# A new searched issue order, MLP partial sums split by token group, and dense matmuls in four column tiles, in an attention + token-mixing MLP kernel on one Trainium2 core

## The chip, the cores and the metric

The kernel runs on one core of one Trainium2 chip. The metric is the device time of one execution in microseconds (us). The time before is the median of 3 runs. One further execution was profiled, and its trace is what the numbers below come from.

## The reference, cut to what matters

There are 2048 tokens with 512 channels, in bf16. A vector `c` gives six modulation vectors `sa, ca, ga, sb, cb, gb`. Then:

```python
h = layernorm(x) * (1 + ca) + sa
qkv = h @ wqkv                      # 512 -> 1536; 32 heads of 16
p = softmax(mask(q @ k.T / 4))      # causal, window of 256 tokens
x = x + ga * ((p @ v) @ wo)
h = layernorm(layernorm(x) * (1 + cb) + sb)
u = gelu(h.T @ w1 + b1)             # the MLP mixes tokens: 2048 -> 1792
x = x + gb * (u @ w2 + b2).T        # 1792 -> 2048
```

The MLP contracts over tokens. Its first product needs the rows of all 2048 tokens, but a part of the sum over tokens can be formed as soon as those tokens have left attention.

## The kernel before, in words

**Groups.** Tokens are handled in four groups G of 512 (four tiles of 128). For each group: layer norm, projection to queries, keys and values (`proj0`, `proj`), attention (`attention`), output projection, residual and the two layer norms (`post`), which leave the tiles `hb`, the input of the MLP.

**Attention.** There are 75 chunks (`chunks`). A chunk is one group of score matmuls on TensorE (tiles `pss` and `psb`, in four row tiles of 32), two exponentials on ScalarE (`et<-pss` over 1536 columns and `et<-psb` over 512), and masks on VectorE (`et<-et,maskt`). The tile `pss` has one buffer, so the scores of a chunk wait until the long exponential of the chunk before is done. When all chunks of a unit (8 heads, 256 queries) are there, `sums` issues the value sums and the sums of the weights (`po`, 52 matmuls for most units), each matmul in one of four column tiles of 32 (tile form 128*32). `finish` takes the logarithm and the exponential of the sums (`lz`, ScalarE) and multiplies (`OT`, VectorE).

**Dense matmuls** use the full array (128*128) and 512 columns: projections (`pk`, `pq`, `pv`), output projection (`pa`), first MLP product (`pu`, in the program also `pu2`), second MLP product (`py`). In the planner a change between row tiles, column tiles and the full array costs `SWITCH` = 0.107 us, by the class `cls` of an operation.

**MLP.** `w1` has 14 column blocks `fc` of 128, loaded in pairs. `partials` sums each of the 14 blocks over the token tiles 0 to 7 (eight matmuls into one PSUM tile) once groups 0 and 1 have left `post`, and copies the sum into `part`. `tail` and `mlp1` then add the token tiles 8 to 15 (`pu2`, 8 matmuls for each block, 112 in all). Eight PSUM tiles are open at a time, so blocks 8 to 13 start when earlier ones have been emptied. Then come gelu and the second product: 16 output tiles with 14 matmuls each (`py`). This kernel's first eight token tiles of a pair of blocks are one load of 512 KB (`w1p`), the other eight a second one (`load_w1(pair, 1)`, operation `w1h`) into the same buffer, once the partial sums that read the first are done. The 14 loads of `w2` (`e_w2`, 512 KB each, tiles `w2r`) start when attention's buffers are released.

**Order.** Every operation is an `Op` with an engine, a planned cost and dependencies. `run_schedule` issues all of them in the order of the list `ORDER` (L60), with engines from `CHOSEN` (L114); issue order is the program order of each engine. All loads but three early ones are issued by SyncE (SP). The operation `w2` has a planned cost of 0.0 and issues its 14 loads in a row.

**Opening.** TensorE runs 16 matmuls of zeros (`warm`, written into `pss`) around the modulation matmuls (`ps_fm`) and the transposes of the first two token tiles, before the first key projection.

All operations are recorded through one helper, so the profile gives them line L234, and they are told apart by their tiles.

Of the kernel before, what the change touches and what calls it, by code (L numbers as in the profile page):

```python
# [9 lines left out]
ACT = mybir.ActivationFunctionType  # L10
# [3 lines left out]
P = 128  # L14
# [12 lines left out]
PART_A = 3  # L27
PART_AT = 20.0
# [3 lines left out]
X_READY = [3.0, 3.75, 11.7, 12.0]  # L32
MOD_READY = [4.7, 6.7, 6.9, 7.4]
W_READY = [8.35, 9.25, 9.25, 11.0, 14.0]
# [17 lines left out]
ZSCALE = 2.0 ** -32  # L52

# [59 lines left out]
]  # L113
CHOSEN = {  # L114
    "ACT": [
        48, 50, 72, 74, 95, 1017, 1034, 1039,
    ],
    "DVE": [
# [4 lines left out]
    ],  # L123
    "POOL": [
        712, 714,
    ],
}
BATCH = True
XT_AFTER = -0.7
W1_AFTER = 2.0  # L130
AV_POS = 0.2
LZ_POS = 0.0
# [4 lines left out]
class Op:  # L137
# [5 lines left out]
    def __init__(self, name, eng, cost, emit, deps=(), pos=0.0, cls=None, alloc=None, ready=0.0, extra=0.0, behind=()):  # L143
# [5 lines left out]
        self.done = None  # L149
        Op.count += 1  # L150
        self.n = Op.count

# [1201 lines left out]
```

## Time and profile before

| | us |
|---|---|
| median of 3 runs | 255.73 (255.32 to 256.43) |
| profiled execution, its own time | 258.61 |
| its span, first to last instruction | 256.8 |
| TensorE busy | 241.1 (94% of the span), 3427 matmuls |
| ScalarE busy | 179.9 (70%) |
| VectorE busy | 200.6 (78%) |
| GpSimd busy | 133.0 (52%) |
| mean granted TensorE clock | 0.993 |

The span has an opening up to 12.5 us, attention with ScalarE busy nearly throughout until about 175 us, and a last stage to 256.8 us in which TensorE runs dense matmuls without a break. Matmuls overlap, so their durations (380 ns) are longer than the step from one to the next; steps are read from their starts.

### The profile page before, as it was taken

The numbers are of one execution on the slowest core, as the hardware profiler recorded it, in microseconds if no ns is written. First come the engines' busy times: TensorE is split into PE (matmuls) and PEld (weight loads), VectorE is DVE, ScalarE is ACT, GpSimd is POOL, SyncE is SP. The second block draws the span as 40 slices with busy tenths as digits, with TensorE's granted clock in tenths as the row PEclk, the third lists the DMA queues.
The fourth block names the chain that finished last, engine by engine and source line by source line (L and its number), as shares of the span: only waits on it lengthen the run. The fifth ranks groups of instructions, "written<-read, shape, count | busy, mean of one in ns | idle before, by whom it ended". The sixth has DMA issues, their size and how long they took to land.

```text
span 256.8 us, 8133 instructions
## 1 busy us (share of the span) xinstructions
PE 241.1 (94%) x3427; PEld 122.2 (48%) x3427; DVE 200.6 (78%) x392; ACT 179.9 (70%) x255; POOL 133.0 (52%) x237
## 2 busy tenths in 40 slices
PE   7988989899998999979999999999999999999994
PEld 2665635444443454434545454446444444444443
DVE  4589999998899999998658879799869864444442
ACT  4399999999999999998999999998138510000000
POOL 8288977999999897896914389190000000000000
PEclk9999999999999999989999999999999999999999
DMA  7998360246254400060030003351899601111111
GB/s 222 326 349 252 12 80 3 42 114 159 61 120 60 116 3 3 9 182 0 5 92 14 3 3 84 106 142 37 326 332 387 232 22 41 58 48 41 41 43 41
DMA packets 41341, 27.02 MB, mean 105 GB/s; under 512 B 11992, under 2 KB 37208, under 8 KB 41304
## 3 DMA queue, kind: packets, MB, share of 16 engines
q1 hardware_dynamic: 41008, 25.97, 36.2%
q8 instruction: 27, 0.44, 0.7%
q10 hardware_dynamic: 296, 0.53, 0.6%
q14 instruction: 10, 0.08, 0.1%
HBM read 22.03 MB, written 2.10 MB: 94 GB/s over the span
## 4 chain that ended last, share of the span: by engine, by line
PE 61%; POOL 12%; DVE 10%; ACT 8%; issue 4%; DMA 3%; SPq 0%; DVEq 0%; POOLq 0%
PE pu L234 20%; PE py L234 19%; PE po L234 7%; ACT et L234 6%; PE pss L234 6%; POOL VT L234 4%; PE pa L234 3%; DVE et L234 3%; POOL xn L234 3%; POOL KT L234 2%; PE pk L234 2%; DMA w1p<-in_B_w_dram 2%; PE pv L234 2%; ACT lz L234 1%; DVE vb L234 1%
## 5 line engine op out<-in xcount | busy, mean ns | idle before, releaser
L234 ACT ACTIVATE et<-pss 128x1536 bf16<-128x1536 f32 x75 | 110.8, 1477 | 3.3 <-PE psb L234 1.7
L234 PE MATMUL pu<-hb,w1p 128*128 128x512 bf16 x224 | 52.6, 380 | 0.0
L234 DVE TENSOR_TENSOR et<-et,maskt 128x1024 bf16<-128x1024 bf16 (+2 forms) x79 | 48.5, 628 | 2.7 <-ACT et L234 2.6
L234 PE MATMUL py<-guT,w2r 128*128 128x512 bf16 (+1 forms) x238 | 48.7, 366 | 0.5 <-DVE otile L234 0.5
L234 ACT ACTIVATE et<-psb 128x512 bf16<-128x512 f32 x75 | 46.9, 626 | 0.0
L234 PE MATMUL pss<-QT,KT 32*128 32x64 bf16 (+3 forms) x720 | 30.0, 232 | 6.6 <-ACT et L234 5.0
L234 PEld LDWEIGHTS <-w2r 128*128 128x128 bf16 x238 | 23.3, 98 | 26.0 <-issue 0.7
L234 PE MATMUL po<-et,VT 128*32 128x64 bf16 (+3 forms) x960 | 32.3, 237 | 1.0 <-DVE kb L234 0.6
L234 PEld LDWEIGHTS <-w1p 128*128 128x128 bf16 x224 | 20.4, 98 | 25.0 <-issue 2.5
L234 PE MATMUL po<-et,ones_bd 128*32 128x256 bf16 (+3 forms) x624 | 32.0, 271 | 0.0
L234 POOL TENSOR_SCALAR KT<-kb,mask_par 128x512 bf16<-128x512 bf16 (+1 forms) x38 | 27.4, 732 | 7.2 <-ACT kb L234 5.8
L234 DVE TENSOR_TENSOR otile<-py,xr 128x512 bf16<-128x512 f32 (+1 forms) x17 | 11.2, 660 | 25.3 <-PE py L234 25.2
L234 PEld LDWEIGHTS <-KT 32*128 32x128 bf16 x960 | 15.8, 93 | 31.1 <-issue 28.9
L234 PE MATMUL psb<-QT,KT 32*128 32x64 bf16 (+3 forms) x240 | 29.5, 232 | 0.0
L234 PEld LDWEIGHTS <-VT 128*32 128x32 bf16 x960 | 19.6, 97 | 12.9 <-issue 10.7
L234 POOL TENSOR_SCALAR xn<-x,rs,nm 128x512 bf16<-128x512 bf16 x24 | 22.8, 951 | 1.4 <-DVE h L234 0.5
L234 DVE BATCH_NORM_STATS2 st<-x 128x6 f32<-128x512 bf16 x32 | 21.4, 682 | 2.2 <-DMA x<-in_A_x_dram 2.1
L234 PE MATMUL pk<-h1T,wqkv 128*128 128x256 bf16 (+2 forms) x108 | 21.3, 326 | 0.6 <-DVE vb L234 0.5
L234 PEld LDWEIGHTS <-wqkv 128*128 128x128 bf16 x164 | 13.8, 99 | 13.4 <-issue 6.0
L234 DVE TENSOR_TENSOR OT<-po,lz 128x256 bf16<-128x256 f32 x32 | 13.3, 416 | 8.2 <-ACT lz L234 8.2
L234 PE MATMUL pv<-wqkv,h1T 128*64 128x256 bf16 (+1 forms) x112 | 17.2, 321 | 0.4 <-DVE OT L234 0.4
L234 PE MATMUL pa<-wod,OT 128*128 128x512 bf16 x64 | 17.0, 380 | 0.4 <-DVE kb L234 0.2
(99 smaller groups left out, 324.1 us busy)
## 6 DMA issues: line engine op xcount, KB each, us to landing
w1p<-in_B_w_dram SPq DMA_DIRECT2D x14, 512.0 KB, 5.0
w2r<-in_B_w_dram SPq DMA_DIRECT2D x14, 512.0 KB, 7.8
x<-in_A_x_dram SPq DMA_DIRECT2D x16, 128.0 KB, 5.2
wmod<-in_w_mod_dram SPq DMA_DIRECT2D x4, 512.0 KB, 8.6
out_dram<-otile SPq DMA_DIRECT2D x15, 128.0 KB, 1.7
wqkv<-in_A_wqkv_dram SPq DMA_DIRECT2D x4, 256.0 KB, 4.9
vs<-vb SPq DMA_DIRECT2D x24, 32.0 KB, 3.0
wmod<-in_w_mod_dram ACTq DMA_DIRECT2D x2, 256.0 KB, 3.7
```

Of the source, the lines that this page charges most:

```text
L234: ins = call(*args, **kwargs)
```

## The change

1. **Order.** `ORDER` and `CHOSEN` are new lists. The planned costs of many operations on VectorE and GpSimd are lower (0.77 for 0.88 of a normalization on GpSimd). More operations can go to either engine: `kk`, `vp`, `vo`, `xn`, `n2` and `hb`. In the program this moves 8 normalizations `xn`, 6 `hb`, 8 copies into `VT` and 6 splits into `KT` from GpSimd to VectorE, and 6 scalings of `h1T` and 6 multiply or add steps of `h` the other way.
2. **Partials by token groups.** For the first `EARLY` = 10 blocks `fc`, the token tiles 0 to 3 are summed first and copied into `part` (`pe`); later the tiles 4 to 7 are summed and added (`pd`, VectorE, 10 new additions). Blocks 10 to 13 still sum eight tiles at once. `w1` is loaded in 28 quarters of 256 KB (tiles `w1s`, `w1r`) in place of 14 halves.
3. **Four column tiles.** Dense operations of the stage get the class of the value sums. Those in a run of at most `NEAR_RUN` = 7 operations beside a value sum are issued by `mm` as four matmuls of 32 columns, 163 dense matmuls in all (652 small ones).
4. **Smaller edits.** 12 warming matmuls for 16, ten of them at the very start; the first transposed tiles are both copied by ScalarE; the zeros of `VT[2]` are two SP transfers instead of four GpSimd fills.

The diff, cut to its core (`ORDER` and `CHOSEN` are left out):

```diff
+    runs = []
+    for o in (ops[i] for i in ORDER if "PE" in ops[i].engs):
+        if not runs or runs[-1][0].cls != o.cls:
+            runs.append([])
+        runs[-1].append(o)
+    for run in runs:
+        sums = [n for n, o in enumerate(run) if o.name == "AV"]
+        if run[0].cls == "AV" and sums:
+            for a, b in zip([-1] + sums, sums + [len(run)]):
+                if b - a <= NEAR_RUN:
+                    for o in run[a + 1 : b]:
+                        o.tiled = True
...
+    def mm(dst, lhsT, rhs, start, stop):
+        if not Op.quad:
+            te.matmul(dst, lhsT=lhsT, rhs=rhs, start=start, stop=stop, skip_group_check=True)
+            return
+        for j in range(4):
+            rows = slice(32 * j, 32 * j + 32)
+            te.matmul(
+                dst[rows], lhsT=lhsT[:, rows], rhs=rhs, start=start, stop=stop, tile_position=(0, 32 * j), skip_group_check=True,
+            )
...
-    warms = [op("warm", "PE", 0.86 if i < 4 else 0.43, lambda e, i=i: e_warm(e, 2, i == 0), pos=-7, cls="D", ready=1.4 if i < 4 else 4.8)
-             for i in range(8)]
+    warms = [op("warm", "PE", 0.86, lambda e: e_warm(e, 2), pos=-7, cls="D", ready=1.4) for i in range(6)]
...
+    def load_w1(pair, quarter):
+        first = quarter in (0, 2) or (quarter == 1 and pair < EARLY // 2)
+        name = f"w1{'s' if first else 'r'}{pair}"
+        t = box["w1" if first else "B"].tile([P, 4, 2 * P], BF, name=name, tag=name)
+        dma.dma_start(out=t[:], in_=w1_v[:, 4 * quarter : 4 * quarter + 4, 2 * P * pair : 2 * P * (pair + 1)])
+        w1t[pair, quarter] = t
...
+        for fc in range(EARLY):
+            pos = start_of(2) + EARLY_AT + fc * EARLY_STEP
+            early[fc] = group(fc, 0, [loads[fc // 2, 0], *done[:4]], pos, True)
+            if fc % 2:
+                load(fc // 2, 1, [early[fc - 1], early[fc]], pos + 0.5)
...
+            if fc < EARLY:
+                g = group(fc, 4, [loads[fc // 2, 1], *done[4:]], pos, False)
+            else:
+                g = group(fc, 0, [loads[fc // 2, 0], loads[fc // 2, 1], *done], pos, True)
             part_ops.append(g)
-            if fc % 2 == 1:
-                second[fc // 2] = op("w1h", "SP", 1.35, lambda e, fc=fc: load_w1(fc // 2, 1), deps=[g], pos=pos + 0.5, extra=W1_AFTER)
+            if fc % 2:
+                second[fc // 2] = [
+                    load(fc // 2, 2, part_ops[-2:], pos + 0.5),
+                    load(fc // 2, 3, [released] + (part_ops[-2:] if fc >= EARLY else []), max(pos, start_of(NG) - 10.0) + 0.6),
+                ]
...
-                o = op("u", "PE", 0.431, e_u, deps=done[sc : sc + 2] + prev + guard + [part_ops[PART_A], second[fc // 2]],
-                       pos=pos + (later if sc == NT - 2 else 0.01), cls="D", alloc="od" if kind == "od" and sc == lo else None)
+                o = op("u", "PE", 0.431, e_u, deps=done[sc : sc + 2] + prev + guard + second[fc // 2],
+                       pos=pos + (later if sc == NT - 2 else 0.01), cls="AV", alloc="od" if kind == "od" and sc == lo else None)
```

More of the change, by code (lines that the diff above doesn't have):

```diff
@@ L26 @@
 NPART = 14
-PART_A = 3
-PART_AT = 20.0
+EARLY = 10
+EARLY_AT = 6.0
+EARLY_STEP = 1.4
 KQ_AT = -3.0
@@ L284 @@
     nc.gpsimd.memset(ones_bd[KB:P, DH : 2 * DH], ZSCALE)
+    nothing = const.tile([P, D], BF, name="nothing")
+    nc.vector.memset(nothing[:], 0.0)
     late = ctx.enter_context(tc.tile_pool(name="late", bufs=2))
@@ L310 @@
     modw = tc.alloc_tile_pool(name="modw", bufs=1, side="right")
-    warm = modw.tile([P, D], BF, name="warm")
-    nc.vector.memset(warm[:], 0.0)
+    warm = nothing
     wmod = modw.tile([P, ND, 6 * D], BF, name="wmod")
@@ L439, with e_warm @@
     box = {}
-    def e_warm(e, n, first):
+    def e_warm(e, n):
         if "warm" not in box:
@@ L492, with dense @@
     fms[0].frees = [o_fm]
-    def dense(name, pieces, emit, deps, pos, cls="D", alloc=None, ready=0.0):
+    fms[1].deps += warms
+    def dense(name, pieces, emit, deps, pos, cls="AV", alloc=None, ready=0.0):
         first = None
@@ L523, in e_bce @@
                 ve.tensor_copy(out=dst[:], in_=box["bc", v][:])
[L525 removed]
+        a, z = dense(f"bc{v}", [0.435] * 2, e_bc, [o_rep], 9.0 + n, cls="D", alloc="od", ready=22.0)
         b = op(f"bce{v}", "DVE", 0.6, e_bce, deps=[z], pos=9.0 + n)
@@ L625, in normed @@
                 o.ready = X_READY[i]
-            xn_ops = [op("xn", "DVE", 0.33, lambda e, i=i: e_xn(e, i), deps=[st], pos=base + 0.5) for i in own]
+            xn_ops = [op("xn", "DVE", 0.36, lambda e, i=i: e_xn(e, i), deps=[st], pos=base + 0.5) for i in own]
             def e_tr(n):
@@ L672, in e_hh @@
                         e_h(e, 2 * i + 1)
-                    hs[half].append(op("h1T", {"ACT": 0.94, "DVE": 0.7}, 0.9, e_hh, deps=[z, o_fm], pos=base + 1.5))
+                    hs[half].append(op("h1P", {"ACT": 0.94, "DVE": 0.7}, 0.9, e_hh, deps=[z, o_fm], pos=base + 1.5))
                     a.frees = hs[half][-1:]
@@ L730, in e_mm @@
                     w0 = (1 - n) * D + g8 * P
-                    te.matmul(
-                        box["kq", g8][:, n, :], lhsT=wqkv[:, dc, w0 : w0 + P], rhs=h1T[:, dc, cols],
-                        start=(dc == 0), stop=(dc == ND - 1), skip_group_check=True,
+                    mm(
+                        box["kq", g8][:, n, :], wqkv[:, dc, w0 : w0 + P], h1T[:, dc, cols],
+                        (dc == 0), (dc == ND - 1),
                     )
@@ L810, in proj0 @@
             f(p)
-        zeros[2] = [
-            op("z", "POOL", 0.93, lambda e, n=n: po.memset(VT[2][:, 2 * n : 2 * n + 2, :, :], 0.0), deps=k_done[0, 1][-1:], pos=1.0 + n)
-            for n in range(4)
-        ]
+        zeros[2] = []
+        for n in range(2):
+            zeros[2].append(op("z2", "SP", 2.6, lambda e, n=n: dma.dma_start(
+                out=VT[2][:, 4 * n : 4 * n + 4, :, :].rearrange("p b a d -> p b (a d)"),
+                in_=nothing[:].unsqueeze(1).to_broadcast([P, 4, D]),
+            ), deps=zeros[2] + k_done[0, 1][-1:], pos=14.0 + n, ready=30.0, extra=1.0))
         proj_last[0] = op("fence", "SP", 0.0, lambda e: None, deps=last, pos=13.0, extra=-2.0)
@@ L866, in e_q @@
                 for dc in (2 * n, 2 * n + 1):
-                    te.matmul(
-                        box["q", g8][:], lhsT=wqkv[:, dc, g8 * P : (g8 + 1) * P], rhs=h1T[:, dc, :],
-                        start=(dc == 0), stop=(dc == ND - 1),
+                    mm(
+                        box["q", g8][:], wqkv[:, dc, g8 * P : (g8 + 1) * P], h1T[:, dc, :],
+                        (dc == 0), (dc == ND - 1),
                     )
@@ L886, in e_k @@
                 for dc in (2 * n, 2 * n + 1):
-                    te.matmul(
-                        box["k", g8][:], lhsT=wqkv[:, dc, D + g8 * P : D + (g8 + 1) * P], rhs=h1T[:, dc, :],
-                        start=(dc == 0), stop=(dc == ND - 1),
+                    mm(
+                        box["k", g8][:], wqkv[:, dc, D + g8 * P : D + (g8 + 1) * P], h1T[:, dc, :],
+                        (dc == 0), (dc == ND - 1),
                     )
@@ L924, in e_v @@
                 for dc in (2 * n, 2 * n + 1):
-                    te.matmul(
-                        box["v", tb][:], lhsT=h1T[:, dc, tb * P : (tb + 1) * P], rhs=wqkv[:, dc, 2 * D : 3 * D],
-                        start=(dc == 0), stop=(dc == ND - 1),
+                    mm(
+                        box["v", tb][:], h1T[:, dc, tb * P : (tb + 1) * P], wqkv[:, dc, 2 * D : 3 * D],
+                        (dc == 0), (dc == ND - 1),
                     )
@@ L956, in v @@
             vx = op("vx", "SP", 1.05, e_vx, deps=[ve_op], pos=pos, extra=0.1)
-            own = op("vo", "POOL", 0.97, lambda e: e_vp(e, True), deps=[ve_op] + war + zeros[r3], pos=pos)
-            b = op("vp", "POOL", 0.97, lambda e: e_vp(e, False), deps=[vx, own] + war + zeros[r3], pos=pos)
+            own = op("vo", {"POOL": 0.78, "DVE": 0.45}, 0.78, lambda e: e_vp(e, True), deps=[ve_op] + war + zeros[r3], pos=pos)
+            b = op("vp", {"POOL": 0.78, "DVE": 0.45}, 0.78, lambda e: e_vp(e, False), deps=[vx, own] + war + zeros[r3], pos=pos)
             ring("vb", 2, ve_op, b)
@@ L979, in e_wo @@
                 for g in (2 * n, 2 * n + 1):
-                    te.matmul(
-                        box["wo", tl][:], lhsT=OT[r2][g][:, tl * P : (tl + 1) * P], rhs=wod[:, g, :],
-                        start=(g == 0), stop=(g == ND - 1),
+                    mm(
+                        box["wo", tl][:], OT[r2][g][:, tl * P : (tl + 1) * P], wod[:, g, :],
+                        (g == 0), (g == ND - 1),
                     )
@@ L992, in post @@
             a.frees = [x_ops[tl]]
-        engine, shifted = ({"POOL": 0.88}, True) if G < POOL_POST else ({"DVE": 0.33}, False)
+        engine, shifted = ({"POOL": 0.77, "DVE": 0.35}, True) if G < POOL_POST else ({"DVE": 0.34}, False)
         st = norm_ops("l2", lambda i: xres[4 * G + own[i]], [[x_ops[tl]] for tl in own],
@@ L1024, in e_w1 @@
         box["A"] = ctx.enter_context(tc.tile_pool(name="partA", bufs=1, side="right"))
-    def load_w1(pair, half):
-        own = half == 1 and pair >= NPART // 2
-        name = f"w1p{pair}_{half}" if own else f"w1p{pair}"
-        t = box["B" if own else "w1"].tile([P, 8, 2 * P], BF, name=name, tag=name)
-        dma.dma_start(out=t[:], in_=w1_v[:, 8 * half : 8 * half + 8, 2 * P * pair : 2 * P * (pair + 1)])
-        w1t[pair, half] = t
+    def load_w1(pair, quarter):
[4 more added lines that the diff above has]
+        w1t[pair, quarter] = t
     def w1s(sc, fc):
-        return w1t[fc // 2, sc // 8][:, sc % 8, (fc % 2) * P : (fc % 2 + 1) * P]
+        return w1t[fc // 2, sc // 4][:, sc % 4, (fc % 2) * P : (fc % 2 + 1) * P]
     part_ops = []
@@ L1040, in partials, with load, e_rel @@
         opened = op("w1", "SP", 0.0, e_w1, deps=mod_ops + [o_fm, masks_built], pos=start_of(1) + 2.0, extra=-2.0)
-        loaded = []
+        loads = {}
+        chain = []
+        def load(pair, quarter, deps, pos):
+            name = f"w1{'abcd'[quarter]}"
+            o = loads[pair, quarter] = op(name, "SP", 1.3, lambda e: load_w1(pair, quarter), deps=deps, pos=pos, extra=W1_AFTER)
+            return o
+        def e_rel(e):
+            wpool.release()
+            box["B"] = ctx.enter_context(tc.tile_pool(name="partB", bufs=1, side="right"))
@@ L1042, in partials @@
         for n in range(NF // 2):
-            loaded.append(op("w1l", "SP", 2.6, lambda e, n=n: load_w1(n, 0), deps=loaded[-1:] or [opened],
-                             pos=start_of(1) + 3.0 + 2.0 * n, extra=W1_AFTER))
+            chain.append(load(n, 0, chain[-1:] or [opened], start_of(1) + 3.0 + 2.0 * n))
         done = [hb_ops[G][tl] for G in range(2) for tl in range(4)]
-        for fc in range(NPART):
-            at = start_of(2) + PART_AT
-            pos = at + fc * (start_of(NG) - PART_END - at) / NPART
-            def e_p(n, fc=fc):
+        released = op("rel", "SP", 0.0, e_rel, deps=[proj_last[NG - 1]], pos=start_of(NG) - 12.0, extra=-2.0)
@@ L1051, in e_p, with group @@
+        def group(fc, lo, deps, pos, first):
+            hi = 8 if first and fc >= EARLY or not first else 4
+            def e_p(n):
                 if n == 0:
                     box["p", fc] = bank([P, D], F32, "pu")
-                for sc in (2 * n, 2 * n + 1):
-                    te.matmul(
-                        box["p", fc][:], lhsT=w1s(sc, fc), rhs=hb[sc][:], start=(sc == 0), stop=(sc == 7),
-                    )
-            def e_pe(e, fc=fc):
-                if fc == PART_A:
-                    wpool.release()
-                    box["B"] = ctx.enter_context(tc.tile_pool(name="partB", bufs=1, side="right"))
-                    for pair in range(NPART // 2, NF // 2):
-                        load_w1(pair, 1)
-                part[fc] = box["A" if fc < PART_A else "B"].tile([P, D], F32, name=f"part{fc}")
-                copy(e, part[fc][:], box["p", fc][:])
@@ L1067, in partials @@
-            behind = [proj_last[NG - 1]] if fc >= PART_A else []
-            a, z = dense("p", [0.431] * 4, e_p, [loaded[fc // 2]] + done + behind, pos, alloc="od")
-            g = op("pe", {"ACT": 0.5, "DVE": 0.6}, 0.6, e_pe, deps=[z] + part_ops[-1:], pos=pos)
-            a.frees = [g]
-            part_ops.append(g)
-            if fc % 2 == 1:
-                second[fc // 2] = op("w1h", "SP", 1.35, lambda e, fc=fc: load_w1(fc // 2, 1), deps=[g], pos=pos + 0.5, extra=W1_AFTER)
+                for sc in (lo + 2 * n, lo + 2 * n + 1):
+                    mm(
+                        box["p", fc][:], w1s(sc, fc), hb[sc][:], (sc == lo), (sc == hi - 1),
+                    )
@@ new lines, in e_pe @@
+            def e_pe(e):
+                if first:
+                    part[fc] = box["A" if fc < EARLY else "B"].tile([P, D], F32, name=f"part{fc}")
+                    copy(e, part[fc][:], box["p", fc][:])
+                else:
+                    ve.tensor_tensor(out=part[fc][:], in0=box["p", fc][:], in1=part[fc][:], op=ALU.add)
+            a, z = dense("p", [0.431] * ((hi - lo) // 2), e_p, deps, pos, alloc="od")
+            g = op("pe" if first else "pd", {"ACT": 0.5, "DVE": 0.6} if first else "DVE", 0.68, e_pe,
+                   deps=[z] + ([released] if fc >= EARLY else []) + ([] if first else [early[fc]]), pos=pos)
@@ new lines, in group @@
+            a.frees = [g]
+            return g
+        early = {}
+        for fc in range(EARLY):
[3 more added lines that the diff above has]
+                load(fc // 2, 1, [early[fc - 1], early[fc]], pos + 0.5)
+        for pair in range(EARLY // 2, NF // 2):
+            load(pair, 1, [released], start_of(NG) - 11.0 + pair - EARLY // 2)
+        for fc in range(NF):
+            at = start_of(3)
+            pos = at + fc * (start_of(NG) - PART_END - at) / NF
+            if fc < EARLY:
+                g = group(fc, 4, [loads[fc // 2, 1], *done[4:]], pos, False)
+            else:
+                g = group(fc, 0, [loads[fc // 2, 0], loads[fc // 2, 1], *done], pos, True)
+            part_ops.append(g)
+            if fc % 2:
[3 more added lines that the diff above has]
+                ]
```

44 lines of the change are left out of this document (23 added, 21 removed), and 119 rows, old and new, of tables (CHOSEN, ORDER).

## The prediction

> **What bounds the kernel now.** I read the profile by stage: first the chain of work that ended last, in order of time, for the end.
>
> ```profile
> 181.83 22.88 PE pu L234 x106
> 204.71 46.87 PE py L234 x224
> ```
>
> From the last score matmuls on, TensorE is the bound: 112 `pu2` and 238 `py` matmuls must all run there, in program order, and nothing else is late. So whatever holds one of them up delays the end by as much. Next the busy times by stretches (columns: busy time of PE, weight loads, VectorE, ScalarE, GpSimd; then granted clock, share of the DMA engines, GB/s).
>
> ```profile
> 20.00:113.00 93.00, 84.46 (x1655) 43.54 (x1653) 89.33 (x175) 92.31 (x125) 82.56 (x140) 1.00 0.36 75
> 113.00:116.50 3.50, 3.27 (x56) 1.77 (x55) 3.47 (x7) 2.95 (x5) 2.72 (x5) 0.51 0.56 157
> 116.50:172.00 55.50, 54.99 (x995) 27.48 (x994) 44.09 (x79) 54.09 (x74) 33.07 (x55) 1.00 0.20 52
> 178.00:182.00 4.00, 4.00 (x20) 1.86 (x19) 2.98 (x7) 1.19 (x4) 0.00 (x0) 1.00 0.63 217
> 182.00:186.00 4.00, 4.00 (x21) 1.78 (x19) 3.46 (x10) 1.10 (x3) 0.00 (x0) 1.00 0.91 343
> 186.00:190.00 4.00, 4.00 (x20) 1.84 (x19) 3.19 (x9) 1.33 (x3) 0.00 (x0) 1.00 1.11 319
> 190.00:194.00 4.00, 4.00 (x21) 1.79 (x19) 2.47 (x5) 2.22 (x4) 0.00 (x0) 1.00 1.08 366
> 194.00:202.00 8.00, 8.00 (x39) 3.64 (x38) 6.95 (x15) 5.34 (x8) 0.00 (x0) 1.00 1.05 386
> 202.00:204.00 2.00, 2.00 (x11) 0.93 (x10) 1.44 (x5) 0.98 (x2) 0.00 (x0) 1.00 0.45 169
> ```
>
> Up to 113 us ScalarE is busy 92.31 of 93: attention runs at its pace and cannot run faster. From 178 to 203 us the DMA engines are full: the loads of `w2`. Last, SP's own timeline, where the transfers are issued, and the tile `w1p`:
>
> ```profile
> 177.93 2.90 SPq L234 DMA_DIRECT2D w2r<-in_B_w_dram  x5
> 184.88 0.99 SPq L234 DMA_DIRECT2D w1p<-in_B_w_dram  x2
> 185.92 8.25 SPq L234 DMA_DIRECT2D w2r<-in_B_w_dram  x9
> ...
> DMA to landing us min/median/max: 4.0/5.0/7.9
> ```
>
> The last two pieces of `w1` go between the fifth and the sixth load of `w2`. The later of them holds blocks 10 and 11 and is first used by the 67th of the 112 `pu2`, 46 before their end: 204.71 - 46 x 0.2155 = 194.8 us. Issued by 185.87, and landing at most 7.9 later (193.8), it is in time by about 1 us. (0.2155 is the step of dense matmuls: 22.88 / 106 = 0.216.)
>
> **The change, part by part.** All sums are against the profiled span of 256.8; what they give is added to the median of 255.73.
>
> *Order of the transfers.* In the changed program's instruction order SP's last loads stand so:
>
> ```
> w1r6                x1    (last quarter of pair 6)
> w2r0, w2r1          x14
> w1s6                x1    (third quarter of pair 6)
> w1s4                x1    (third quarter of pair 4: blocks 8 and 9)
> ```
>
> On TensorE the 61st `pu2` (block 8, token tile 8) loads `w1s4`. Call T the end of the value sums, when attention's buffers are released (before: 177.77, `w2` issued at 177.93). When is `w1s4` wanted? After T: 6 `pu2` (1.29) and a class switch, about 0.1 until the last `OT` (1.5 in all; before, `pa` started 1.74 after T), 8 `pa` (1.72), 54 `pu2` (11.64): T + 14.9. When does it land? Before, the rows above add up to 8.4 MB, the 14 loads of `w2` and the two of `w1`, the last bytes at 202 + 0.34 MB / 386 = 202.9, which is T + 25.1. After, two pieces of 0.26 MB take the place of two of 0.52, so 0.52 MB less at 319 GB/s, 1.6 us: T + 23.5, and an estimated 0.5 until the counter arrives: T + 24.0. TensorE stands still for 9.1 us, and 52 `pu2` and all `py` are queued behind it. Lower bound, all 7.86 MB at 386 GB/s with the first bytes at T + 1.6: T + 22.0, 7.1 us. Upper bound: `w1r6`, issued just ahead, takes 0.8 us of the same engines and the counter 1 us: 10.4. I take 9.1, from the same transfers of the same stage. Could it be hidden? No: in this stage TensorE has no other work, and its program order is fixed.
>
> *Clock after the standstill.* The granted clock was 0.51 from 113 to 116.5 us, after TensorE had stood idle for 1.72 us; 3.5 us at 0.51 cost 1.7 us of work. After 9 us of standstill the same should come: +1.7, from +0.5 (if it ends early) to +3.4 (two such stretches, an estimate). The Trainium skill, "TensorE: Matmul & The Clock Gate", Part 1, says that the clock is judged in free-running windows of about 3.4 us and returns only after a busy one, so resumed work pays the rest of one window too. By that the term would be up to 3.4 and the sum 266.1; the one stretch here, 3.4 us long, agrees with the window's length.
>
> *Attention.* Switches between row tiles, column tiles and full array fall from 189 to 157 between the first and the last scores, by counting both orders; at 0.11 us (8 `pu` between score groups took 1.83, and 8 x 0.2155 is 1.72) TensorE saves 3.5 us. But ScalarE paces here: 75 long exponentials issued every 1.34 us when queued, 75 short ones at 0.48, 64 `lz` at 0.26 and 0.31; all that stays. What can be won are ScalarE's gaps, the largest 1.27 us at 113.9 and 117.2, in the stretch of half clock, where TensorE had little to do (two score groups with nothing between). The early sums of 40 dense matmuls land around there, so I take half of it and some: -0.8, between -2.0 (gaps gone; the work between successive scores now averages 2.03 us in the last 24 chunks, 2.13 before, where the exponentials need about 2.07) and +1.5 (one such gap elsewhere, as the chunks 30 and 31 now have only 1.30 us of work each).
>
> *VectorE and GpSimd.* The ten added `pd` cost 0.69 each (as `part<-pu`), 6.9 us, in a stage where VectorE is busy 44.09 of 55.50. Normalizations of 0.95 on GpSimd become 0.41 on VectorE, copies of 0.51 about 0.42 (as the 256-column cast into `kb`). Both stay below ScalarE's pace; their risk is in the +1.5. The two SP transfers of zeros and 14 more `w1` issues of 0.4 to 0.6 us stand ahead of exchanges `vs`, which attention needs only a group later; taken at 0.
>
> *Four column tiles.* 52 value-sum matmuls (13 groups of four, 2560 columns in all per tile) took 1.21 with a switch, so 1.10: the groups run side by side at 1.07 us for 2560 columns. 512 columns in four tiles then cost 0.216, as one dense matmul does: 0.
>
> *Opening.* The first key projection started at 10.49, behind six warming matmuls; its input was there at 9.36 (8.50 + 0.86). Without these, 1.1 us could go, less 0.45 for the second copy behind the first on ScalarE: -0.6, at best -1.2 (one projection fewer before the first scores). But up to 10.07 the warming matmuls stepped at 0.43, half rate; if full rate comes later without them, the 16 matmuls ahead of the first scores cost 1 us more and the next ones too: +1.5.
>
> *After the last scores.* 104 value-sum matmuls are left instead of 156, 13 groups of four less (1.1 us), and 132 dense ones for 130 (+0.4): -0.7, up to 0 if `pa` waits.
>
> Sum: -0.6 - 0.8 - 0.7 + 9.1 + 1.7 = +8.7; 255.73 + 8.7 = **264.4** (the profiled span would be 265.5).
>
> **Rivals.** *The load is in time, faster.* If `w1s4` lands before T + 14.9, only -2.1 is left: 253.6. By the rates above 4.5 MB, under nine loads of `w2`, have moved by then, so it would have to pass at least five. Against it: before, the two `w1` pieces behind five loads of `w2` landed up to 7.9 after their issue, though other pieces needed 4.0, so they queued. For it: no row shows a queue of fourteen.
> *It overtakes in part.* SP paused from 180.83 to 184.88 after five loads, so it lets few be open (in the order each waits for a counter used eight loads before). If `w1s4` is issued when the eighth `w2` load is in (T + 13) and needs the median of 5.0, it lands at T + 18: 3.1 us, and a shorter cold stretch: 255.73 - 2.1 + 3.1 + 0.9 = 257.6. The full DMA engines from 186 to 202 speak against it.
> *Column tiles are dear.* If each of the 163 showed one weight load (0.098 us), 16 us more on TensorE, half of it in chunks where ScalarE waits: 264.4 + 8 = 272. Against it: 960 small loads for `po` with the same mean (97 ns), hidden. The Trainium skill, "TensorEngine Tiling (Array Packing)", Restrictions and Gotchas, says that column tiling excludes the fast weight load, which speaks against this part; by this trace the loads of both forms take the same 97 to 98 ns.
>
> **How the numbers follow.** The forecast has 0.84, the partial overtaking 0.07, the load in time 0.04, dear column tiles 0.05. Combining the terms' bounds as independent gives about -3 and +4 around 264.4: 260.8 to 268.3, which holds nine tenths of the forecast's own cases, near 8 in 10 of all. 0.5% (1.3 us) is about what a measurement of this kernel tells from no change. Faster: the load in time, 0.04. Same: the lower edge of the overtaking, 0.03. Slower: 0.93.
>
> **What would show it.** Right: a standstill of TensorE of 7 to 10 us some 15 us after the last value sums, ended by the landing of `w1s4`, a clock near 0.5 behind it, and `py` starting near 214. Right for the rest: no gap of 1 us in ScalarE between 20 and 170, four column tiles of 512 columns stepping at 0.216. Wrong: TensorE without a gap from the last scores to the end, or `w1s4` landing before its `w2` neighbours.

## The result, and the profile after

The changed kernel takes **268.49 us** (median of 4 runs, 268.02 to 269.78), the kernel before 255.9 (255.32 to 256.43): a ratio of 1.05, 95% interval 1.0455 to 1.0546. It is slower, as forecast; the forecast of 264.4 was 4.1 us short, and its range ended 0.2 us below the result. The profiled execution took 268.85 us, with a span of 267.1 us.

TensorE's timeline behind the last value sums (start, duration, group; in square brackets the idle time ahead of the group and what ended it):

```profile
188.22 4.05 PE L256 MATMUL pu<-hb,w1r 128*128 128x512 bf16 x17
202.10 1.89 PE L256 MATMUL pu<-hb,w1s 128*128 128x512 bf16 x4 [9.84 <-DMA w1s<-in_B_w_dram]
203.78 1.06 PE L256 MATMUL pu<-hb,w1r 128*128 128x512 bf16 x2
...
214.87 10.31 PE L256 MATMUL py<-guT,w2r 128*128 128x512 bf16 x46
```

The value sums end at T = 177.41. The `pu` in need of `w1s4` is the next in order at 192.26, which is T + 14.85; it starts at 202.10, T + 24.7. The two `pu` of 203.78 span 1.06 us where a pair spans 0.59 at full clock. SP's queue shows why it waited:

```profile
175.32 0.37 SPq L256 DMA_DIRECT2D w1r<-in_B_w_dram  x1
177.56 12.39 SPq L256 DMA_DIRECT2D w2r<-in_B_w_dram  x14
190.91 3.45 SPq L256 DMA_DIRECT2D w1s<-in_B_w_dram  x2
```

The two late loads are issued at 190.91 and 192.26, over 13 us behind the first of `w2`: in the trace, eight transfers are open at a time, and each further issue comes when the load eight before it has landed (the issue of 192.26 behind a landing at 192.25). The loads of `w2` land one after the other, 1.36 us apart, and `w1s4` lands at 202.05, 9.8 us after its issue. The same stage by stretches (columns as before: TensorE, weight loads, VectorE, ScalarE, GpSimd, then granted clock, DMA share, GB/s):

```profile
180.00:200.00 20.00, 12.21 (x56) 5.39 (x55) 12.94 (x29) 6.83 (x13) 0.00 (x0) 0.88 1.03 373
200.00:202.00 2.00, 0.00 (x0) 0.00 (x0) 0.00 (x0) 0.00 (x0) 0.00 (x0) 0.50 0.15 37
202.00:205.00 3.00, 2.90 (x7) 1.04 (x8) 0.00 (x0) 0.00 (x0) 0.00 (x0) 0.50 0.00 0
205.00:218.00 13.00, 12.95 (x60) 5.93 (x60) 9.58 (x20) 5.78 (x8) 0.00 (x0) 0.99 0.01 3
```

The DMA engines are full (1.03) until about 200 us; in the last 2 us of the wait only the rest of the two late loads moves (0.15). The clock is half from 195.0 (0.88 over 20 us is about 5 us at half) to 205.2: 10.2 us, the last 3.1 of them with work, which cost 1.6.

Last, the end of attention in both kernels, 21 us up to about 1 us before the last long exponential, before and after:

```profile
151.30:172.30 21.00, 21.00 (x338) 9.96 (x330) 19.01 (x34) 20.67 (x29) 14.26 (x20) 1.00 0.40 101
```

```profile
150.00:171.00 21.00, 18.64 (x450) 10.52 (x450) 20.41 (x36) 19.40 (x26) 14.81 (x23) 1.00 0.35 98
```

Before, ScalarE is the full engine (20.67 of 21) and VectorE has 2 us to spare (19.01). After, VectorE is nearly full (20.41), and ScalarE (19.40) waits for TensorE, which in its longest wait there waits for VectorE (shown below).

To compare executions, the span is cut at three events, read from ScalarE's and TensorE's timelines: the start of the first long exponential (`et<-pss`), of the last (the 75th), and of the first `py`. Each line is one profiled execution; the median beside it is of all runs of that kernel.

| kernel | first exponential | first to last exponential | last exponential to `py` | median us |
|---|---|---|---|---|
| before, first profile | 12.89 | 160.40 | 31.25 | 255.9 |
| before, run again | 10.85 | 160.16 | 31.26 | 256.53 |
| changed | 11.50 | 160.55 | 42.82 | 268.49 |
| changed, `w1` ahead of `w2` | 12.24 | 160.59 | 30.70 | 256.88 |
| before, `w1` behind `w2` | 11.04 | 160.00 | 43.75 | 267.91 |
| `w1` ahead, no column tiles | 11.34 | 163.11 | 30.77 | 259.66 |
| addition earlier | 11.15 | 160.37 | 30.43 | 256.80 |
| old opening too | 10.42 | 161.03 | 30.33 | 255.94 |
| changed, `w1` on the other queue | 11.49 | 160.65 | 30.32 | 256.58 |
| changed, `w1` behind eleven | 11.63 | 160.59 | 38.50 | 264.63 |
| changed, other queue, late | 10.93 | 160.80 | 37.53 | 262.97 |
| old opening, `h` on GpSimd | 10.39 | 159.87 | 30.33 | 255.26 |
| same, copy on ScalarE | 10.78 | 160.64 | 31.19 | 255.44 |

### The profile page after: what moved, and what is told of

The parts are those of the page before. It is cut to its first block, busy times and chain, and to the rows that moved or that the text cites. A ratio compares the mean times of both kernels' runs of the same rounds, so it can differ in the third digit from the quotient of the medians.

```text
span 267.1 us, 9109 instructions
## 1 busy us (share of the span) xinstructions
PE 235.7 (88%) x3891; PEld 126.5 (47%) x3915; DVE 209.5 (78%) x418; ACT 179.8 (67%) x255; POOL 120.3 (45%) x217
## 4 chain that ended last, share of the span: by engine, by line
PE 41%; ACT 22%; DVE 17%; DMA 9%; issue 7%; SPq 2%; POOL 0%; DVEq 0%; ACTq 0%; POOLq 0%
ACT et L256 19%; PE py L256 18%; PE pu L256 9%; DVE et L256 5%; PE pss L256 4%; DMA w2r<-in_B_w_dram 4%; DMA w1s<-in_B_w_dram 4%; PE po L256 3%; ACT lz L256 2%; DVE st L256 2%; SPq L256 2%; PE pv L256 2%; PE pk L256 2%; PE pa L256 2%; DMA x<-in_A_x_dram 1%
## 5 line engine op out<-in xcount | busy, mean ns | idle before, releaser
L256 PE MATMUL pu<-hb,w1s 128*32 128x512 bf16 (+1 forms) x289 | 40.7, 385 | 12.5 <-DMA w1s<-in_B_w_dram 9.8
L256 POOL TENSOR_SCALAR KT<-kb,mask_par 128x512 bf16<-128x512 bf16 (+1 forms) x32 | 23.7, 750 | 11.3 <-DVE kb L256 11.0
L256 PEld LDWEIGHTS <-VT 128*32 128x32 bf16 x960 | 21.9, 96 | 13.1 <-issue 4.1
L256 PEld LDWEIGHTS <-w1s 128*32 128x32 bf16 (+1 forms) x296 | 14.5, 98 | 28.5 <-DMA w1s<-in_B_w_dram 10.3
L256 ACT ACTIVATE g<-a,b1FM 128x512 bf16<-128x512 f32 x14 | 9.8, 720 | 17.1 <-DVE guT L256 12.8
L256 PE MATMUL pk<-h1T,wqkv 128*32 128x512 bf16 (+4 forms) x191 | 20.8, 333 | 0.2 <-issue 0.2
L256 DVE TENSOR_TENSOR a<-pu,part 128x512 f32<-128x512 f32 x14 | 9.3, 685 | 13.9 <-PE pu L256 13.9
L256 PEld LDWEIGHTS <-wqkv 128*32 128x32 bf16 (+1 forms) x320 | 14.6, 96 | 11.4 <-issue 3.1
L256 PE MATMUL pv<-wqkv,h1T 128*32 128x512 bf16 (+2 forms) x182 | 17.5, 344 | 1.7 <-DVE OT L256 1.4
L256 PE MATMUL pu<-hb,w1r 128*32 128x512 bf16 (+1 forms) x112 | 18.5, 384 | 0.1
```

The source lines that it names most:

```text
L256: ins = call(*args, **kwargs)
```

## The experiments

**The standstill: place in the queue, or something else of the new order?** First the changed kernel with only its two late loads moved:

```diff
 ORDER:  - ... 719, 934, 1062, 1060, 930, 935, 937, 931, 936, 938, 1036, 1092 ...
         + ... 719, 934, 1060, 1036, 1062, 930, 935, 937, 931, 936, 938, 1092 ...
         # 1062 = w2 (14 loads), 1060 and 1036 = the w1 loads w1s6 and w1s4
```

> The changed kernel with the last two w1 loads (w1s6, w1s4) issued just ahead of the 14 loads of w2, nothing else. Theory (place in SP's queue): the wait of 9.84 us and the 1.6 us lost at half clock behind it go, 268.5 - 11.4 = 257.1; TensorE without a break from the last scores to the end. Rival (the stage has become limited by transfers in general, with 28 smaller loads of w1): another wait for w1 or w2 of several us comes instead, 262 or more. Rival (the column tiles or the new order cost the time): 266 to 268.

Measured: 256.88 (256.13 to 257.51), ratio to the kernel before 0.9999 (0.9973 to 1.0025). 11.6 us are gone, and with them the whole difference; no wait for `w1s` is left on TensorE. Then the other way round: the kernel before, with its last two `w1` loads put behind `w2`.

```diff
 ORDER:  - ... 1040, 949, ... 950, 1029, 1087, 1066, 952, 1079, 1041, 1059 ...
         + ... 949, ... 950, 1087, 1066, 952, 1079, 1041, 1040, 1029, 1059 ...
         # 1041 = w2, 1040 and 1029 = the last two w1h
```

> The kernel before with its last two w1 loads (512 KB each) moved behind the 14 loads of w2, nothing else. Theory: the last of them lands when all 8.4 MB are in, 26.5 us after the end of the value sums, and is wanted at the 67th of 112 pu2 matmuls, 17 us after it: a standstill of 9.5 us, then about 1.6 at half clock: 255.9 + 11 = 267. Rival (loads pass each other): 256 to 258.

Measured: 267.91 (266.65 to 269.71), ratio 1.0435 (1.0384 to 1.0485). The old order with this one fault is as slow as the new one (268.49). From the waits of TensorE:

```profile
PE pu L234 <- DMA w1p<-in_B_w_dram: 9.7, 1, 9.7
```

The clock is half from 197.3 to 207.5 us here, the last 5.3 us of it with work, which cost 2.6.

The unchanged kernel ran beside these:

> The kernel before, unchanged, to see span and granted clock of each execution. The profiled execution had 256.8 span, clock 0.993, with a stretch of 3.4 us at half clock from 113 us and 258.61 in all, 2.9 above the median of 255.73. Theory: that stretch and ScalarE's gaps in it belong to some executions only; the others have a clock nearer 1.0 and a span near 254, so the sum of the prediction, made against the profiled execution, was added to a base 2.9 too low (258.61 + 8.7 = 267.3 would have been the forecast). Rival: all spans are 256 to 257 and only what lies around them differs; then the missing 4 us are in the change itself.

Measured: 256.53 (255.34 to 259.93), ratio 1.0005 (0.9972 to 1.0038). The stretch of half clock inside attention came again in this execution (111.2 to 114.6), and nine of the 12 executions have the same mean clock, 0.993: it is usual in that order. The three at 0.999 or 1.000 are not all faster (255.34 to 258.00). What differs between the two executions of the kernel before is the opening. TensorE's last warming matmuls and the first key projection, in the first profile and in the second:

```profile
7.98 2.72 PE L234 MATMUL pss<-warm 128*128 128x512 bf16 x6
10.49 0.49 PE L234 MATMUL pss<-h1T,wqkv 128*128 128x128 bf16 x4
```

```profile
7.43 1.24 PE L234 MATMUL pss<-warm 128*128 128x512 bf16 x5
8.51 0.39 PE L234 MATMUL pss<-h1T,wqkv 128*128 128x128 bf16 x4
```

The same warming matmuls ran at half rate until 10.5 in the first and at full rate from 7.43 in the second. The first exponential came 2.04 us sooner, and the execution took 256.24 instead of 258.61.

**How the landing depends on the place.** The two late loads behind eleven of the fourteen:

```diff
+                if h == 1 and n == 8:        # after 11 of the 14 w2 loads
+                    box["w1late"][0]()       # w1s6
+                    box["w1late"][1]()       # w1s4
                 dma.dma_start(out=box["w2r"][h][:, fc : fc + 2, :], ...
```

> The changed kernel, but the two late w1 loads stand behind eleven of the fourteen w2 loads instead of all of them. Theory (transfers land in the order of the queue, 0.52 MB each at 319 GB/s, 1.64 us): the landing moves by 3 x 1.64 = 4.9 us, the standstill of TensorE is 9.84 - 4.9 = 4.9 us, the stretch of half clock behind it stays (1.6 us of cost), and the time is 268.5 - 4.9 = 263.6. Rival (a few transfers are open at a time and the small ones pass the big ones): no standstill, 256.9. Rival (TensorE waits for the end of all transfers): 268.5.

Measured: 264.63 (264.46 to 266.09), ratio 1.033 (1.0281 to 1.0379). TensorE and the clock:

```profile
187.44 4.05 PE L256 MATMUL pu<-hb,w1r 128*128 128x512 bf16 x17
196.95 1.89 PE L256 MATMUL pu<-hb,w1s 128*128 128x512 bf16 x4 [5.46 <-DMA w1s<-in_B_w_dram]
```

```profile
191.40:197.00 5.60, 0.14 (x2) 0.05 (x2) 2.75 (x6) 2.77 (x5) 0.00 (x0) 0.85 1.10 357
197.00:199.00 2.00, 2.00 (x5) 0.68 (x6) 0.00 (x0) 0.00 (x0) 0.00 (x0) 0.50 1.00 371
199.00:201.00 2.00, 2.00 (x6) 0.76 (x5) 0.00 (x0) 0.00 (x0) 0.00 (x0) 0.50 0.17 65
201.00:203.00 2.00, 2.00 (x8) 0.78 (x7) 0.21 (x1) 0.00 (x0) 0.00 (x0) 0.72 0.00 0
```

T is 176.64 here, so the wait ended at T + 20.3 instead of T + 24.7: 4.4 us for three loads, 1.46 each (expected 1.64). The wait fell by 4.4 to 5.46, but the time only by 3.9. This shorter standstill cost more clock: half rate from 195.3 to 202.1, of which 5.2 us with work, so 2.6 us and not 1.6. The two together would make 3.4; the profile of the changed kernel has another loss of about 1 us, told below.

**Is it the queue, or the full DMA engines?** The changed kernel, its two late loads issued by ScalarE, on a queue of its own:

```diff
-        dma.dma_start(out=t[:], in_=w1_v[:, 4 * quarter : ...
+        queue = ac if quarter == 2 and pair in (4, 6) else dma
+        queue.dma_start(out=t[:], in_=w1_v[:, 4 * quarter : ...
```

> The changed kernel, nothing moved, but its two late w1 loads are issued by ScalarE on its own queue instead of SP, at the same place in the order. Theory (the place in SP's queue is what costs): they land some 5 to 8 us after their issue, before TensorE wants them at T + 14.9, no standstill, 256.9. Rival (the DMA engines are full, and every transfer waits for what was issued before it, whatever the queue): standstill of about 9.8 us as before, 268.5; sharing that favours neither: between, near 261.

Measured: 256.58 (255.98 to 257.15), ratio 0.9996 (0.9969 to 1.0022). The issue of `w1s4` on ScalarE's queue, and the same place on TensorE:

```profile
179.47 0.44 ACTq L256 DMA_DIRECT2D w1s<-in_B_w_dram  x1
```

```profile
187.35 4.05 PE L256 MATMUL pu<-hb,w1r 128*128 128x512 bf16 x17
191.24 1.03 PE L256 MATMUL pu<-hb,w1s 128*128 128x512 bf16 x4
```

No wait, as the theory said. But the run does not separate the two. ScalarE did not have to stand behind SP's 14 issues and issued `w1s4` already at 179.47; it landed at 188.16, while the loads of `w2` that SP issued at 179.44 and 179.95 landed at 186.17 and 187.94. It landed behind a load that SP issued half a us later: it was in time because it was issued early. A further run issues the two loads on the same queue, but late, when SP has eight loads open:

```diff
 ORDER:  - ... 719, 934, 1062, 1060, 930, ... 938, 1036, 1092, ... 949, 1073 ...
         + ... 719, 934, 1062, 930, ... 938, 1092, ... 949, 1036, 1060, 1073 ...
         # 949 = the third pair of rs (layer norm) on ScalarE; the two loads still on ScalarE's queue
```

> The run with the two late w1 loads on ScalarE's queue did not separate the two theories: ScalarE issued the needed one at 179.47, when SP had issued only four or five of its 14 w2 loads, and it landed at 188.16, between two w2 loads issued half a us before and half a us after it. Here ScalarE issues them behind its third pair of rs operations, not before 187.4, with some eight w2 loads open on SP's queue (w1s4 first). It may also have to wait for an earlier load's counter, to about 191. Theory now (what is issued earlier lands earlier, whatever the queue): it lands about 10 us after its issue, at 198 to 201, TensorE stands still for 6 to 9 us, and the time is 264 to 267.5. Rival (a queue of its own is served in turn with the other): it lands 4 to 5 us after its issue, at 192 to 195.5, standstill 0.5 to 4, and the time is 257.5 to 262.

Measured: 262.97 (262.56 to 263.25), ratio 1.0248 (1.0196 to 1.03), between the two ranges of time. ScalarE's queue and TensorE:

```profile
187.04 0.95 ACTq L256 DMA_DIRECT2D w1s<-in_B_w_dram  x2
```

```profile
195.37 1.89 PE L256 MATMUL pu<-hb,w1s 128*128 128x512 bf16 x4 [4.38 <-DMA w1s<-in_B_w_dram]
```

`w1s4`, issued at 187.04 without a further wait, landed at 195.33, after 8.3 us: inside the rival's range of landings (192 to 195.5), not the theory's (198 to 201). The loads that SP issued at 185.30 and 186.60 landed at 194.04 and 195.87. The second one, issued at 187.47, needed 11.4 us and landed behind a load that SP issued half a us later. The packets that the two queues moved between 191 and 194 us show what happened (q1 is SP's queue, q10 ScalarE's; number of packets, MB, share of the DMA engines):

```profile
q1 hardware_dynamic: 451, 0.87, 81.8%
q10 hardware_dynamic: 439, 0.22, 26.6%
```

The two queues are served in turn, about one packet of each: in this the rival is right, and it is not so that only the time of issue counts, whatever the queue. But a packet of `w1` carries a quarter of the bytes of one of `w2`, so `w1s4` got a fifth of what moved. Its 0.26 MB took from 190.8 to 194.4, and its first packet moved only 3.7 us after the issue. What held the first packet is open. The Trainium skill, "DMA: Bandwidth & Descriptors", Queues, rings and completion order, says that a DMA engine takes turns between the queues that have work for it. The packets of this run agree; even so the lone load of 0.26 MB landed only half a us ahead of the 0.52 MB that SP had issued half a us before it. The other queue also saves the time that SP needs to get to the issue.

**Column tiles.** The kernel with `w1` ahead, and all dense matmuls on the full array again:

```diff
-NEAR_RUN = 7
+NEAR_RUN = 0
```

> As e1_w1_ahead_of_w2, with no dense matmul in column tiles (NEAR_RUN = 0), same order. Theory (512 columns in four tiles cost one dense step, and ScalarE paces attention): TensorE pays some 80 to 100 switches more of 0.11 us between the scores, of which the chunks with slack hide most: 0 to 4 us slower than e1. Rival (column tiles are dear): faster than e1 by 3 us or more.

Measured: 259.66 (259.18 to 260.25), ratio 1.0114 (1.0075 to 1.0154), 2.8 us slower than with tiles. In the table the loss is all between the first and the last exponential, 163.11 against 160.59, in steps of 0.1 to 0.35 us at seventeen chunks, not at one place. So four column tiles are a gain in this order (an order searched for the full array was not tried), and the rival that feared their weight loads fails: those of `w1s` have a mean of 97 ns with tiles and 98 without.

**Where did the gain of the column tiles go?** In the new order one gap of ScalarE stood out: chunk 68 (counted from 0), where TensorE waited 1.70 us for one of the added `part` additions on VectorE:

```profile
157.54 1.89 PE L256 MATMUL pu<-hb,w1s 128*128 128x512 bf16 x7 [1.70 <-DVE part L256]
```

In the kernel with `w1` ahead, that addition and the next were put ahead of the `h` operations (of a layer norm) on the same engine:

```diff
 ORDER:  - ... 704, 1026, 857, 1020, 833, 841, 706, 1023, 1027, 834, 858, 860, 1013, 1024, 1030 ...
         + ... 1026, 857, 1020, 833, 841, 1027, 1023, 834, 858, 860, 1013, 1024, 704, 706, 1030 ...
         # 1027, 1024 = additions (pd); 704, 706 = the h operations
```

> The changed kernel with the two w1 loads ahead of w2 (256.88 us), and on VectorE the two additions for the partials of blocks 10 and 12 or so (the ones around chunk 67) ahead of the two h operations that stood before them. Theory: the 1.55 us gap of ScalarE at chunk 68 comes from TensorE's wait of 1.70 us for the added addition, which stood behind a mask operation slowed to 1.37 us; with the addition earlier the gap is gone and the time is 255.4. Rival: something else is late next (TensorE has only 2.7 us to spare in that stretch), the gap opens again one or two chunks later, and the time stays at 256.9.

Measured: 256.80 (255.65 to 258.11), ratio 1.0005 (0.9976 to 1.0035): no change. The long exponentials of chunks 67 to 71, without the edit and with it:

```profile
155.99 1.47 ACT L256 ACTIVATE et<-pss 128x1536 bf16<-128x1536 f32 x1
159.80 1.45 ACT L256 ACTIVATE et<-pss 128x1536 bf16<-128x1536 f32 x1 [1.55 <-PE psb L256]
161.77 1.45 ACT L256 ACTIVATE et<-pss 128x1536 bf16<-128x1536 f32 x1
164.16 1.46 ACT L256 ACTIVATE et<-pss 128x1536 bf16<-128x1536 f32 x1
166.12 1.45 ACT L256 ACTIVATE et<-pss 128x1536 bf16<-128x1536 f32 x1
```

```profile
155.03 1.47 ACT L256 ACTIVATE et<-pss 128x1536 bf16<-128x1536 f32 x1
157.15 1.48 ACT L256 ACTIVATE et<-pss 128x1536 bf16<-128x1536 f32 x1
159.36 1.45 ACT L256 ACTIVATE et<-pss 128x1536 bf16<-128x1536 f32 x1 [0.24 <-PE pss L256]
162.08 1.45 ACT L256 ACTIVATE et<-pss 128x1536 bf16<-128x1536 f32 x1
164.81 1.45 ACT L256 ACTIVATE et<-pss 128x1536 bf16<-128x1536 f32 x1 [0.79 <-PE psb L256]
```

The step at chunk 68 falls from 3.81 to 2.12, and the next three grow by 0.24, 0.33 and 0.77: the rival was right, and the gap moved. VectorE is busy 20.23 of the 21 us from 150 to 171 in this run; moving one operation does not shorten its queue, and the wait is passed on.

**The opening.** On that kernel, the opening of before:

```diff
-    warms = [op("warm", ..., lambda e: e_warm(e, 2), ...) for i in range(6)]
+    warms = [op("warm", ..., lambda e, i=i: e_warm(e, 4 if i == 5 else 2), ...) for i in range(6)]
-    fms[1].deps += warms
+    fms[1].deps += warms[:5]      # the last four warming matmuls behind the modulation
# ORDER starts as before; the copy 45 is done by VectorE again
```

> The kernel of the run before, with the opening as it was before the change: 8 warming matmuls ahead of the transposition of silu instead of 10, 2 among the loads' work and 4 between the modulation and the first key projection (where TensorE stood idle for 0.77 us), and the first copy of the two into h1T on VectorE again. Theory: the changed opening costs 0.7 to 1.4 us (first long exponential at 11.5 and 12.2 us against 10.85 in the kernel before), so this gives about 1.0 less than the run before it: 254.4. Rival: the start depends on when the clock comes up in an execution and not on the order, and the time is within 0.4 of the run before it; with 4 matmuls at half rate it could even be 0.9 later.

Measured: 255.94 (255.48 to 256.93), ratio 0.9985 (0.996 to 1.001). The first exponential comes 0.73 us sooner, but the eleventh only 0.08 sooner (33.83 against 33.91): the second scores now wait, and ScalarE gets through its queue no faster. The medians differ by 0.86, and the ranges overlap.

The granted clock on record tells the executions apart. In the run before, seven of 12 executions have a mean clock of 0.987 to 0.993 and a median of 257.25; the other five, at 1.000, have 255.92. With the old opening all 12 are at 0.999 or 1.000, with 255.94. So the old opening does not shorten an execution whose clock stays up; what it gains is that none of these executions has a lower clock (in the two later kernels with it, one of 24). Where the clock falls is shown by the trace of the kernel with `w1` ahead, which has the new opening (0.993 in that execution); below it the same stretch with the old opening:

```profile
8.40:11.70 3.30, 2.75 (x16) 1.86 (x15) 2.16 (x8) 1.37 (x4) 0.00 (x0) 0.50 1.12 322
8.40:11.70 3.30, 3.22 (x41) 2.58 (x41) 2.15 (x8) 1.91 (x3) 0.00 (x0) 1.00 1.13 321
```

After it had come up once, the clock was half again for these 3.3 us. That it falls at this place in the other executions too is likely but not shown.

**Is VectorE the bound at the end of attention?** Two runs take work from it there:

```diff
 CHOSEN["POOL"]:  + 708            # one pair of h operations (DVE before)
 # second run, in addition
 CHOSEN["DVE"]:   - 1042           # one copy into part
 CHOSEN["ACT"]:   + 1042
```

> The kernel with the old opening (255.94 us), and one pair of h operations (1.5 us near chunk 69) on GpSimd instead of VectorE. Theory: in the last 21 us of attention VectorE has become the bound (busy 20.45 of 21 after the change, 19.02 before it, while ScalarE fell from 20.41 to 19.38), so 1.5 us less there lets the steps at chunks 69 to 71, which are 1.3 us over those of the kernel with the gap, shrink: 255.0 (between 254.6 and 255.6). Rival: GpSimd's operation slows VectorE's mask operations beside it by as much (0.68 became 1.35 and more), and the time stays at 255.9.

Measured: 255.26 (254.57 to 256.81), ratio 0.9945 (0.9912 to 0.9979). The last stretch of attention:

```profile
150.00:171.00 21.00, 20.12 (x489) 11.19 (x492) 20.14 (x37) 20.65 (x30) 18.27 (x24) 1.00 0.36 102
```

ScalarE is full again (20.65, as before the change), GpSimd rose to 18.27, and the step at chunk 71 fell from 2.73 to 1.95. From first to last exponential it is 159.87, the shortest of the table. This version is faster than the kernel before by about half a per cent, more than its interval. Against the run with the old opening alone (255.94) the gain is 0.7 us, and there the intervals of the two ratios overlap; the step at chunk 71 is the firmer evidence.

> The run before, and one copy of a partial sum (0.68 us on VectorE) on ScalarE (about 0.6). Theory: VectorE is the bound in that stretch and ScalarE has some 1 us to spare, so another 0.3 to 0.6 comes off: 254.6. Rival: ScalarE is as full as VectorE, and its 0.6 us moves the exponentials behind it: 255.5 to 256.0, no better than the run before.

Measured: 255.44 (254.84 to 256.59), ratio 0.9959 (0.993 to 0.9988), faster than the kernel before too, but no better than the run before it. The rival holds: with ScalarE at 20.65 of 21, 0.6 us more for it gains nothing.

## Why the prediction was right or wrong

**Right: the mechanism of the standstill, and nearly both of its terms.** The loads behind `w2` cost 9.1 + 1.7 = 10.8 in the sum. The profile shows 9.84 and 1.6; undoing only this takes 11.6 off the median (11.9 with the second queue). The place of the standstill was right to a tenth (wanted at T + 14.85, predicted T + 14.9); the wait ended 0.7 later than T + 24.0, as the upper bound allowed. These 0.7 lie in the last bytes: the sum let the last 0.34 MB of the old kernel move at 386 GB/s, up to T + 25.1, while its own row has 169 GB/s there, and the last load of `w2` landed at 204.29, T + 26.5. Less the 1.6 for the smaller pieces, this gives T + 24.9, close to what was measured. The 0.5 until the counter arrives, for which the prediction had no row, fits: the last packet ended at 201.52 and the counter came at 202.05. Undone, in part, and brought into the old order, it answered each time: 256.88, 264.63 and 267.91. What the text took for its reason, the order of SP's queue, is in part the time of the issue: with eight loads open, SP could not issue `w1s4` before 192.26. On a queue of its own it was served in turn with the loads of `w2`, not behind them.

**Wrong: the sum of the small gains, -2.1, above all the steps *Opening* and *Attention*.** Without the standstill the changed kernel is not 2.1 us faster than before but equal: 0.9999 (0.9973 to 1.0025) and 0.9996 (0.9969 to 1.0022); the three terms measured give +0.6 + 0.4 - 0.8 = +0.2. That is most of what is missing; 0.7 of the standstill is the next part, and 0.2 to 0.8 the base, since the kernel before had medians of 255.9 to 256.5 in later runs against the 255.73 that the sum was added to. By terms:

- *Opening, -0.6:* typical is about +0.6. Seven executions with the new opening have the first exponential at 10.93 to 12.24 (median 11.49), five of six with the old one (or nearly) at 10.39 to 11.04. The step took the one profile of before, where the first key projection started at 10.49 behind warming matmuls at half rate, as typical; it was the exception, 258.61 us against a median of 255.73, a warning that the text gave (the sum is made against the span and added to the median) and did not draw. Profile against that profile the opening gained 1.39; against the second it lost 0.65. The step's own risk, matmuls at half rate ahead of the first scores, came in one of the seven: in the execution that starts at 12.24 the clock was half from 8.4 to 11.8.
- *Attention, -0.8:* +0.4 (160.55 to 160.80 in five executions of the new order, 160.00 to 160.40 in three of the old one). The gap of the half-clock stretch went, as expected, but chunk 68 opened another: counted from the first exponential, and against the second profile of before, the changed kernel is 0.8 behind at chunk 47, 0.8 ahead at 48, 1.0 ahead at 67 and 0.7 behind at 68. (The 1.27 of the prediction is two gaps of ScalarE, 0.21 and 1.06; the gain at chunk 48 is 1.7.) The step named VectorE's 6.9 us of additions and took 0 for them, as busy 44.09 of 55.50 left room; in the last 21 us there was not that room (19.01 of 21 before, 20.41 after), and an average over 55 us hid it.
- *After the last scores, -0.7:* right. From the last exponential to `py` the new order without the standstill needs 30.32 to 30.70, the old one 31.25. In the changed kernel's own profile another 1.1 us was lost there ahead of the standstill; the runs with that part of the order unchanged do not show it, and its cause is open.

**Column tiles, 0:** the cost of the tiles themselves is as said, but they are worth 2.8 us by the run without them. So the rest of the new order, the partial sums among it, costs about as much in attention as the tiles bring: without tiles it takes 163.11 where the old order takes 160.2. How this splits between the partial sums and the order itself was not separated.

## What to carry to other kernels

Follow each load that must be in time to its issue and its landing: the loads that are open when it is issued decide when it lands, and a planner that counts 14 loads as 0.0 sees neither. When a gain is read from fuller engines, look at the second-fullest engine in the very stretch, for it can take over the bound. And before a sum is made from one profiled execution, compare its own time with the median: a difference of 1% sits somewhere in that profile and must be found first.

## What the runs showed of the hardware that had not been expected

- **A second queue is served in turn, packet by packet, and a load of small packets still waits.** From 191 to 194 us the DMA engines moved 451 packets of SP's queue and 439 of ScalarE's, but 0.87 MB against 0.22. `w1s4` took 8.7 and 8.3 us to land on ScalarE's queue, 3.9 and 3.7 of them before its first packet, and 9.8 on SP's.
- **A shorter standstill can cost more clock.** Half clock lasted 10.2 us with standstills of 9.84 and 9.73, and 6.8 with 5.46 and 4.38: three and two times 3.4, the length of the one stretch in the kernel before. Work resumed 3.1, 5.3, 5.2 and 5.4 us before its end, so it cost 1.6, 2.6, 2.6 and 2.7 us. The Trainium skill, "TensorE: Matmul & The Clock Gate", Part 1, gives free-running windows of about 3.4 us; both lengths agree, and by that rule the cost depends on where in a window the work resumes, not on the length of the wait.
- **The start of the clock differs between executions.** The same opening ran its warming matmuls at half rate to 10.5 us in one execution and at full rate from 7.4 in another; the first exponential moved by 2.04 us and the whole execution by 2.4.
